# Linear attention feeding a squared-ReLU MLP on one core: the front of the kernel reordered and its loads and stores spread over three queues

## Chip, cores and metric

One Trainium2 chip, one of its cores. The metric is device time in microseconds of one execution; the kernel before takes 1178.36 us (median of 3 runs, 1177.33 to 1179.15). What is said of stages comes from one profiled execution.

## What is computed

For each of 8 batches and 8 heads (sequence 576, head dimension 64, float32):

```
kv  = k^T v                                  # 64 x 64 for each head
o   = q kv;   o = o / sqrt(mean(o^2) + 1e-6) * g_norm
x   = o, heads side by side                  # 4608 tokens x 512
out = (s * relu(x @ w_in)^2 + b) @ w_out     # 512 -> 2048 -> 512
```

w_in (512 x 2048) and w_out (2048 x 512) arrive as 64-bit floats: the kernel reads each as two 32-bit words and makes a float32 of it. Because b is one number, the part of it that reaches the output is b times the column sums of w_out.

## The kernel before, in words

The 4608 tokens are 36 chunks of 128; four chunks make a unit, so there are 9 units. Four groups of two batches (g = 0 to 3) share one pair of kv tables each; a group has 9 chunks, so groups begin at chunks 9, 18 and 27, which belong to the attention that is worked out beside units 1, 3 and 5.

**Attention of a chunk** (`attention`, L277) has three steps: `turn` transposes q on TensorE (L286) and ScalarE copies it out of PSUM (L288); `product` multiplies by the block-diagonal kv (L295), then squares (ScalarE L304), sums (VectorE L306), takes the root (L308), inverts (L310) and scales (L312); `turn_x` transposes the result (L320) into xT (L323). `x_sums` (L329) makes four sums of quarters of xT. `kv_product` (L253) multiplies k and v of a pair of heads in 64 x 64 pieces (L262); after the fourth pair ScalarE copies the kv into `bd_kv` (L273). `load_kv` (L89) loads k and v of a head with two DMAs each, all on SP's queue, into a pool of four buffers for k and four for v; `load_q` (L99) loads two chunks of q with four DMAs.

**The two multiplications** of a unit use Strassen-Winograd products, seven in place of eight: quarters and sums of quarters on both sides. The first one (`mm1`, L364) runs over four blocks s of w_in, with seven slots each: x1, z2, x6, y7, x5, x3, y4; each slot is four matmuls, which the trace shows as eight records, and slots x3 and y4 of a block come between the slots of the next block, so that 26 slots form the stretch and the last two follow later. ScalarE and VectorE evict the banks (L161, L362, L374, L406, L407). The second one (`mm2`, L432) has 14 slots (seven products times two row blocks), reads the seven combinations of w_out from DRAM through a ring of three 1 MB buffers (`load_w2`, L424) and stores the output rows (L459).

**The weights.** `load_w` (L116) brings a block of two 128-row (or 128-column) strips of w into one of two raw buffers, with two DMAs of 512 KB on SP's queue. `round_w` (L133) converts a block: ScalarE scales the high words (L148) and the low words (L149); VectorE then shifts the high words and masks the sign away (L151), puts the sign back (L155) and adds the low words (L158). `make_w_in(s)` (L169) converts two blocks and makes three sums, which stay in SBUF. `make_w_out(s)` (L200) converts two blocks into `up` and `dn` (one buffer each), makes four differences (one of them, t3, in the place of a quarter of `up`), adds the block's rows to `wsum` (L161) and stores the seven combinations to DRAM (L220, SP's queue). When all four blocks are done, `bias_row` (L244) multiplies wsum by b on TensorE. `send_w` (L546) loads the next raw block in a fixed order: w_in's blocks, then w_out's.

**The order** is written out by hand, and each engine and each DMA queue works its own list in that order. At the start (L551 to L569): two raw blocks of w, k and v of heads 0 to 3, q of two chunks, k and v of heads 4 to 7, q of two more chunks, four kv pairs, w_in's block s = 0, attention of chunks 0 to 3, x_sums. Then the units (L592): unit 0 converts w_in's blocks s = 1, 2, 3 after slots 0, 6 and 12 of the first multiplication (L630) and all of w_out, s = 0 to 3, between its two multiplications (L620), then loads the ring. The side work (`side_of`, L571), attention for the next unit's chunks and, in units 1, 3 and 5, the four kv pairs in one piece, is spread over the second multiplication's slots by a due time (L614). The loads of heads 0 to 3 of a new group go out at the start of the unit that needs them (L616), those of heads 4 to 7 after the first and second pair (L637).

## Time and profile before

| what | value |
|---|---|
| time, median of 3 runs | 1178.36 us |
| the profiled execution: time, span | 1181.61 us, 1179.8 us |
| granted TensorE clock, mean | 0.939 |
| busy: TensorE, VectorE, ScalarE, GpSimd | 1010.7, 480.9, 203.4, 2.5 us |
| DMA: moved, mean rate | 128.86 MB, 109 GB/s |
| HBM read, written | 111.15 MB, 16.78 MB |

How to read the lines shown further on. A line of a timeline gives the start in us, the length, the engine, the line of the kernel, the operation, output <- input, the shape and how many instructions are merged (x16), and in brackets how long the engine had idled and what ended that. SPq, ACTq and POOLq are the issuing of DMAs by SyncE, ScalarE and GpSimd: their length is that of the issue and not of the transfer. A line of windows gives for each stretch its length, the busy time of PE (matmul), PEld (weight load), DVE (VectorE), ACT (ScalarE) and POOL (GpSimd) with the number of instructions, the granted TensorE clock, the mean busy share of the 16 DMA engines and the rate. A line of groups gives total busy time, mean ns of one, then the idle time before them with its releaser. A line of waits gives total us, how often, and the longest. A float32 matmul shows as two records.

### The profile page before, as it was taken

What the parts mean: (1) busy time and instruction counts of PE and PEld (TensorE: products, weight loads), DVE (VectorE), ACT (ScalarE), POOL (GpSimd) and SP (SyncE); (2) the same over time, 40 slices, a digit from 0 to 9 for tenths busy, and PEclk for the clock granted to TensorE, in tenths of its full rate; (3) what the DMA queues carried; (4) which work ended last, traced back from release to release, by engine and by line L of the source; (5) the groups of instructions that cost most, each with busy time, mean ns of one, the idle gap of its engine ahead of it and who ended that gap; (6) DMA issues with size and microseconds to landing.
All of it is one profiled execution on the core that took longest, in us unless ns stands there. A gap on an engine that the chain in (4) does not pass through costs nothing.

```text
span 1179.8 us, 14111 instructions
## 1 busy us (share of the span) xinstructions
PE 1010.7 (86%) x6050; PEld 869.3 (74%) x6050; DVE 480.9 (41%) x765; ACT 203.4 (17%) x338; POOL 2.5 (0%) x8
## 2 busy tenths in 40 slices
PE   2588100799978999999979999998699999999998
PEld 2467100688867888888768888887588888888887
DVE  0469565234431355244414452443044534433541
ACT  0353221011101111111111111111011111111100
POOL 0000000000000000000000000000000000000000
PEclk9999655799998999999979999999799999999999
DMA  7434445336133401270245023602350234034022
GB/s 219 138 90 143 130 147 177 151 108 204 55 103 122 142 37 72 81 219 31 81 143 179 1 77 129 197 9 99 117 178 1 81 126 116 16 127 144 1 74 104
DMA packets 79855, 128.86 MB, mean 109 GB/s; under 512 B 43056, under 2 KB 55344, under 8 KB 71728
## 3 DMA queue, kind: packets, MB, share of 16 engines
q1 hardware_dynamic: 79344, 127.95, 33.5%
q8 instruction: 48, 0.79, 0.3%
q14 instruction: 15, 0.12, 0.0%
q10 hardware_dynamic: 448, 0.00, 0.0%
HBM read 111.15 MB, written 16.78 MB: 108 GB/s over the span
## 4 chain that ended last, share of the span: by engine, by line
PE 76%; DVE 10%; SPq 5%; DMA 5%; issue 2%; ACT 2%; DVEq 0%; ACTq 0%
PE x_ps L84 42%; PE y_ps L84 23%; PE z_ps L84 5%; SPq L93 4%; PE x_ps L295 3%; PE xT_ps L320 2%; DVE a L164 2%; DMA w_raw<-in_moe_w_out_dram 2%; PE qT_ps L286 1%; DMA v_sb<-in_v_dram 1%; PE kv_ps L262 1%; DVE wsum L161 1%; DVE xn L312 1%; SPq L220 1%; DVE ss L306 1%
## 5 line engine op out<-in xcount | busy, mean ns | idle before, releaser
L84 PE MATMUL x_ps<-w_sb,a 128*128 128x256 f32 x864 | 200.6, 386 | 9.7 <-DMA w_sb<-w 9.7
L84 PEld LDWEIGHTS x_ps<-w_sb,a 128*128 128x128 f32 x864 | 164.3, 193 | 35.6 <-issue 13.8
L84 PE MATMUL y_ps<-w_sb,a 128*128 128x256 f32 x720 | 162.5, 381 | 0.0
L84 PEld LDWEIGHTS y_ps<-w_sb,a 128*128 128x128 f32 x720 | 135.1, 191 | 17.5 <-issue 0.2
L84 PE MATMUL y_ps<-xs,wb 128*128 128x256 f32 x576 | 136.4, 380 | 0.7 <-DVE a L161 0.7
L84 PE MATMUL x_ps<-xs,ws 128*128 128x256 f32 x576 | 136.2, 379 | 0.0
L374 ACT COPY r<-x_ps 128x512 f32<-128x512 f32 x108 | 63.2, 585 | 343.7 <-PE x_ps L84 338.8
L84 PEld LDWEIGHTS x_ps<-xs,ws 128*128 128x128 f32 x576 | 109.4, 190 | 15.2 <-ACT r L374 0.4
L84 PEld LDWEIGHTS y_ps<-xs,wb 128*128 128x128 f32 x576 | 109.0, 191 | 15.6 <-DVE a L161 1.1
L161 DVE TENSOR_TENSOR a<-y_ps,r 128x512 f32<-128x512 f32 x72 | 49.5, 687 | 130.4 <-ACT r L374 130.4
L444 DVE SCALAR_TENSOR_TENSOR or<-x_ps,s_col,b_row 128x256 f32<-128x256 f32 x54 | 26.1, 484 | 148.3 <-PE x_ps L84 148.3
L262 PE MATMUL kv_ps<-v_sb,k_sb 64*64 64x64 f32 x1152 | 40.0, 279 | 49.9 <-DMA v_sb<-in_v_dram 49.7
L362 DVE SCALAR_TENSOR_TENSOR a<-a 128x512 f32<-128x512 f32 x108 | 74.7, 692 | 3.7
L262 PEld LDWEIGHTS kv_ps<-v_sb,k_sb 64*64 64x64 f32 x1152 | 34.3, 187 | 55.8 <-issue 43.0
L84 PE MATMUL z_ps<-xT,wa 128*128 128x256 f32 x288 | 70.1, 387 | 4.5 <-DVE a L161 4.5
L306 DVE TENSOR_REDUCE ss<-sq 128x8 f32<-128x512 f32 x36 | 24.6, 684 | 120.9 <-ACT sq L304 120.9
L84 PE MATMUL x_ps<-xT,wa 128*128 128x256 f32 x288 | 69.6, 385 | 0.0
L84 PE MATMUL b_ps<-wsum,b_sq 128*128 128x512 f32 x2 | 2.1, 1140 | 77.9 <-DVE wsum L161 77.9
L84 PE MATMUL x_ps<-w_sb,s 128*128 128x256 f32 x288 | 68.5, 393 | 0.0
L84 PE MATMUL x_ps<-xT,ws 128*128 128x256 f32 x288 | 68.0, 379 | 0.0
L84 PEld LDWEIGHTS z_ps<-xT,wa 128*128 128x128 f32 x288 | 55.7, 194 | 13.5 <-DVE a L161 5.7
L84 PEld LDWEIGHTS x_ps<-w_sb,s 128*128 128x128 f32 x288 | 55.5, 197 | 8.7 <-issue 1.2
(65 smaller groups left out, 797.4 us busy)
## 6 DMA issues: line engine op xcount, KB each, us to landing
w_sb<-w SPq DMA_DIRECT2D x63, 1024.0 KB, 4.9
k_sb<-in_k_dram SPq DMA_DIRECT2D x64, 144.0 KB, 2.9
v_sb<-in_v_dram SPq DMA_DIRECT2D x64, 144.0 KB, 3.0
q_sb<-in_q_dram SPq DMA_DIRECT2D x72, 128.0 KB, 4.8
out_dram<-o SPq DMA_DIRECT2D x36, 256.0 KB, 2.2
w_raw<-in_moe_w_in_dram SPq DMA_DIRECT2D x16, 512.0 KB, 4.7
w_raw<-in_moe_w_out_dram SPq DMA_DIRECT2D x16, 512.0 KB, 6.3
w<-w_t SPq DMA_DIRECT2D x12, 256.0 KB, 3.2
```

The costliest lines, as they stand in the source:

```text
L84: nc.tensor.matmul(o, lhsT=lhsT, rhs=rhs, start=start, stop=stop, skip_group_check=True)
L93: nc.sync.dma_start(out=t[s * HB : s * HB + HB].rearrange("p j d -> p (j d)"), in_=src[2 * g + s, h].rearrange("(p j) d -> p (j d)", j=R),)
L161: nc.vector.tensor_tensor(out=o, in0=a, in1=b, op=ALU.add)
L164: nc.vector.tensor_tensor(out=o, in0=a, in1=b, op=ALU.subtract)
L220: nc.sync.dma_start(out=w2_dram[i][:, 2 * s : 2 * s + 2, :], in_=src)
L262: nc.tensor.matmul(kv_ps[g][s][l * HB : l * HB + HB, p, :], lhsT=kt[rows, j, :], rhs=vt[rows, j, :], start=(j == 0), stop=(j == R - 1),)
L295: nc.tensor.matmul(ps[half, p, :], lhsT=st["qT"][:, p, half], rhs=bd[:, s, p, :], start=True, stop=True,)
L306: nc.vector.reduce_sum(ss, sq, axis=mybir.AxisListType.X)
L320: nc.tensor.transpose(ps[:, p, :], st["xn"][:, 2 * p : 2 * p + 2, :], ident)
L362: nc.vector.scalar_tensor_tensor(t, t, 0.0, t, ALU.max, ALU.mult)
L374: nc.scalar.copy(st[name], src)
L444: nc.vector.scalar_tensor_tensor(o, ps, s_col, other, ALU.mult, ALU.add)
```

## The change

- **Conversion.** The scaling of the high words becomes a Prelu whose slope for negative numbers makes the scaled number positive and sets, after VectorE's shift, the sign bit. VectorE's mask and the operation L155 go.
- **Column sums.** VectorE no longer adds up wsum. `bias_row` multiplies each row strip of `up` and `dn` by b on TensorE as soon as it is converted and accumulates in one PSUM bank (16 matmuls of 128 x 512 instead of one).
- **w_out.** Block s = 0 is converted inside unit 0's first multiplication, after slot 18 (x5 of s = 2); s = 1 to 3 after its end. The seven stores go out on GpSimd's queue, two of them after the upper block, five after the lower.
- **w_in.** Upper and lower blocks of s = 0 are converted among the attention of chunks 2 and 3; those of s = 1 to 3 after slots 0, 4 and 11.
- **Start.** k of all eight heads first on SP's queue, v on ScalarE's, into a pool of their own that is given back for `gp` afterwards; then q, a raw block, q, a raw block. The products of chunks 0 to 3 use the banks of the first multiplication.
- **Later units.** The side work has fixed slots. The kv pairs of units 1, 3 and 5 stand after slots 4, 9, 14 and 19 of the first multiplication. Heads 0 to 3 are loaded one unit ahead; unit 0 puts its q loads and these kv loads after the last raw block and ahead of the ring's first load.

```diff
     qp = ctx.enter_context(tc.tile_pool(name="qp", bufs=2))
     attp = ctx.enter_context(tc.tile_pool(name="attp", bufs=2))
     xp = ctx.enter_context(tc.tile_pool(name="xp", bufs=2))
-    gp = ctx.enter_context(tc.tile_pool(name="gp", bufs=NS))
     rp = ctx.enter_context(tc.tile_pool(name="rp", bufs=2))
     dram = ctx.enter_context(tc.tile_pool(name="dram", bufs=1, space=bass.MemoryType.DRAM))
     ps_t = ctx.enter_context(tc.tile_pool(name="ps_t", bufs=2, space=bass.MemoryType.PSUM))
...
     kv_in, q_in, w_raw = {}, {}, {}
-    def load_kv(g, h):
-        for name, src in (("k", k), ("v", v)):
-            t = kvp.tile([P, R, D], FP32, name=f"{name}_sb", tag=name)
+    def load_kv(g, h, pool=kvp, queues=(nc.sync, nc.sync)):
+        for name, src, queue in zip("kv", (k, v), queues):
+            t = pool.tile([P, R, D], FP32, name=f"{name}_sb", tag=name)
             for s in range(2):
-                nc.sync.dma_start(
+                queue.dma_start(
                     out=t[s * HB : s * HB + HB].rearrange("p j d -> p (j d)"),
                     in_=src[2 * g + s, h].rearrange("(p j) d -> p (j d)", j=R),
                 )
...
         raw = w_raw.pop(i).rearrange("p b n -> p (b n)")
         dst = dst.rearrange("p b n -> p (b n)")
         if not wide:
             nc.vector.tensor_copy(out=dst, in_=raw)
             return
-        hi = raw.bitcast(FP32).rearrange("p (n two) -> p n two", two=2)[:, :, 1]
-        lo = raw.rearrange("p (n two) -> p n two", two=2)[:, :, 0]
-        nc.scalar.activation(hi, hi, AF.Copy, scale=2.0**-112)
+        pairs = raw.rearrange("p (n two) -> p n two", two=2)
+        hi, lo = raw.bitcast(FP32).rearrange("p (n two) -> p n two", two=2)[:, :, 1], pairs[:, :, 0]
+        nc.scalar.activation(hi, hi, AF.Prelu, scale=2.0**-112, alpha=-(2.0**32))
         nc.scalar.activation(lo, lo, AF.Copy, scale=2.0**-29)
-        yb, db = raw.rearrange("p (n two) -> p n two", two=2)[:, :, 1], dst.bitcast(U32)
+        db = dst.bitcast(U32)
         nc.vector.tensor_scalar(
-            out=db, in0=yb, scalar1=3, scalar2=0x7FFFFFFF,
-            op0=ALU.logical_shift_left, op1=ALU.bitwise_and,
-        )
-        nc.vector.scalar_tensor_tensor(
-            db, yb, 0x80000000, db, ALU.bitwise_and, ALU.bitwise_or
+            out=db, in0=pairs[:, :, 1], scalar1=3, scalar2=None, op0=ALU.logical_shift_left
         )
         nc.vector.tensor_tensor(out=db, in0=db, in1=lo, op=ALU.add)
...
     wa, wb, ws = {}, {}, {}
-    def make_w_in(s):
-        wa[s] = wp.tile([P, 2, DM], FP32, name=f"wa_{s}")
-        wb[s] = wp.tile([P, 2, DM], FP32, name=f"wb_{s}")
+    def round_w_in(s, lower):
+        store, base = (wb, FC // 2) if lower else (wa, 0)
+        store[s] = wp.tile([P, 2, DM], FP32, name=f"w{'ab'[lower]}_{s}")
+        round_w(base + 2 * s, store[s])
+    def sum_w_in(s):
         ws[s] = wp.tile([P, 3, 2, HN], FP32, name=f"ws_{s}")
-        round_w(2 * s, wa[s])
-        round_w(FC // 2 + 2 * s, wb[s])
         a11, a12 = wa[s][:, :, :HN], wa[s][:, :, HN:]
         a21, a22 = wb[s][:, :, :HN], wb[s][:, :, HN:]
         s1, s2, s4 = (ws[s][:, i] for i in range(3))
         add(s1, a21, a22)
+        sub(s2, s1, a11)
         sub(a21, a11, a21)
-        sub(s2, s1, a11)
         sub(s4, a12, s2)
     def w_in_of(i, s, b, c):
...
     w2_dram = {i: dram.tile([P, FC // 2, HN], FP32, name=f"w2_{i}") for i in range(1, 8)}
-    wsum = const.tile([P, DM], FP32, name="wsum")
     def make_w_out(s):
         up = convp.tile([P, 2, DM], FP32, name="w_up", tag="up")
         dn = convp.tile([P, 2, DM], FP32, name="w_dn", tag="dn")
         t = convp.tile([P, 3, 2, HN], FP32, name="w_t", tag="wt")
-        round_w(FC + 2 * s, up)
-        round_w(FC + FC // 2 + 2 * s, dn)
         b11, b12 = up[:, :, :HN], up[:, :, HN:]
         b21, b22 = dn[:, :, :HN], dn[:, :, HN:]
         t1, t2, t4 = (t[:, i] for i in range(3))
         t3 = b12
+        def keep(*which):
+            for i, src in which:
+                nc.gpsimd.dma_start(out=w2_dram[i][:, 2 * s : 2 * s + 2, :], in_=src)
+        round_w(FC + 2 * s, up)
+        bias_row(up, s == 0, False)
         sub(t1, b12, b11)
-        if s == 0:
-            nc.vector.tensor_copy(out=wsum, in_=up[:, 0])
-        for m, b in ((up, 0), (up, 1), (dn, 0), (dn, 1)):
-            if (s, b) != (0, 0) or m is dn:
-                add(wsum, wsum, m[:, b])
-        sub(t3, b22, b12)
+        keep((1, b11), (5, t1))
+        round_w(FC + FC // 2 + 2 * s, dn)
+        bias_row(dn, False, s == NS - 1)
         sub(t2, b22, t1)
         sub(t4, b21, t2)
-        for i, src in ((1, b11), (2, b21), (6, t2), (7, t3), (5, t1), (3, b22), (4, t4)):
-            nc.sync.dma_start(out=w2_dram[i][:, 2 * s : 2 * s + 2, :], in_=src)
+        sub(t3, b22, b12)
+        keep((2, b21), (6, t2), (3, b22), (4, t4), (7, t3))
     ident = const.tile([P, P], FP32, name="ident")
...
     nc.vector.tensor_scalar(out=b_sq, in0=b_sq, scalar1=b_col, scalar2=None, op0=ALU.mult)
     b_row = const.tile([P, DM], FP32, name="b_row")
-    def bias_row():
-
-        ps = ps_t.tile([P, DM], FP32, name="b_ps", tag="t")
-        matmul(ps, b_sq, wsum, True, True)
-        nc.scalar.copy(b_row, ps)
+    b_ps = []
+    def bias_row(w, first, last):
+        if first:
+            b_ps.append(ps_t.tile([P, DM], FP32, name="b_ps", tag="t"))
+        for b in range(2):
+            matmul(b_ps[0], b_sq, w[:, b], first and b == 0, last and b == 1)
+        if last:
+            nc.scalar.copy(b_row, b_ps[0])
     kv_ps = {}
...
     xT = {}
-    def attention(c):
+    def attention(c, first=False):
         bd = bd_kv[c // R % 2]
...
             nc.scalar.copy(st["qT"], ps)
         def product():
-            ps = ps_a.tile([P, NP, P], FP32, name="x_ps", tag="x")
+            if first:
+                ps = bank_of("att", "xy"[c % 2]).rearrange("p b (m n) -> p (b m) n", m=2)
+            else:
+                ps = ps_a.tile([P, NP, P], FP32, name="x_ps", tag="x")
             for p in range(NP):
                 for s in range(2):
                     half = slice(s * HB, s * HB + HB)
...
             load_w(blocks[sent[0]])
             sent[0] += 1
-    for _ in range(2):
-        send_w()
-    for h in range(4):
-        load_kv(0, h)
+    kv0p = tc.alloc_tile_pool(name="kv0p", bufs=H)
+    for h in range(H):
+        load_kv(0, h, kv0p, (nc.sync, nc.scalar))
     load_q(0)
-    for h in range(4, H):
-        load_kv(0, h)
+    send_w()
     load_q(2)
+    send_w()
     for p in range(NP):
         kv_product(0, p)
-    make_w_in(0)
+    kv0p.release()
+    gp = ctx.enter_context(tc.tile_pool(name="gp", bufs=NS))
+    turn, product, turn_x = zip(*(attention(c, True) for c in range(4)))
+    turn[0]()
+    turn[1]()
+    product[0]()
+    turn[2]()
+    product[1]()
+    turn[3]()
+    turn_x[0]()
+    round_w_in(0, False)
     send_w()
+    product[2]()
+    turn_x[1]()
+    product[3]()
+    turn_x[2]()
+    round_w_in(0, True)
     send_w()
-    first = [attention(c) for c in range(4)]
-    for n in range(6):
-        for i in range(2, -1, -1):
-            if 0 <= n - i < 4:
-                first[n - i][i]()
+    turn_x[3]()
     x_sums(0)
+    sum_w_in(0)
     def side_of(u):
         if u + 1 >= U:
-            return []
-        chunks = range(4 * u + 4, 4 * u + 8)
-        todo = []
-        for c in chunks:
-            if c % R == 0:
-                todo.append([lambda p=p, g=c // R: kv_product(g, p) for p in range(NP)])
-            todo += [[a] for a in attention(c)]
-        todo.append([lambda: x_sums(u + 1)])
-        return todo
-
-    def side_loads(u):
+            return {}
+        turn, product, turn_x = zip(*(attention(c) for c in range(4 * u + 4, 4 * u + 8)))
+        return {
+            2: [turn[0]],
+            3: [product[0]],
+            4: [turn[1]],
+            5: [turn_x[0], product[1]],
+            6: [turn[2]],
+            7: [turn_x[1], product[2]],
+            8: [turn[3]],
+            9: [turn_x[2], product[3]],
+            11: [turn_x[3]],
+            12: [lambda: x_sums(u + 1)],
+        }
+    kv_due = {c // 4 - 1: c // R for c in range(R, CH, R)}
+    def loads(u):
         if u + 1 < U:
-            c = 4 * u + 4
-            load_q(c)
-            load_q(c + 2)
-
-    kv_due = {c // 4 - 1: c // R for c in range(R, CH, R)}
+            load_q(4 * u + 4)
+            load_q(4 * u + 6)
+        if u + 1 in kv_due:
+            for h in range(4):
+                load_kv(kv_due[u + 1], h)
     for u in range(U):
+        if u > 0:
+            loads(u)
         steps = [mm1(u, s) for s in range(NS)]
         slots = []
         for s in range(NS):
...
             if b:
                 slots.append(b["y4"])
             slots += [a["x6"], a["y7"], a["x5"]]
-        m1 = len(slots)
-        second = mm2(u)
-        slots += [second[0], steps[-1]["x3"], steps[-1]["y4"]] + second[1:]
-        side_loads(u)
-        todo = side_of(u)
-
-        at = [0.0]
-        for n in range(len(slots)):
-            at.append(at[-1] + (2.0 if n > m1 + 2 else 1.0))
-        lo, hi = at[m1 + 2], 0.95 * at[-1]
-        due = [lo + (hi - lo) * i / max(1, len(todo) - 1) for i in range(len(todo))]
-        done = 0
-        if u in kv_due:
-            for h in range(4):
-                load_kv(kv_due[u], h)
         for n, slot in enumerate(slots):
-            if u == 0 and n == m1:
-                for s in range(NS):
-                    make_w_out(s)
+            slot()
+            if u == 0:
+                if n in (0, 4, 11):
+                    s = (0, 4, 11).index(n) + 1
+                    for lower in (False, True):
+                        round_w_in(s, lower)
+                        send_w()
+                    sum_w_in(s)
+                if n == 18:
+                    make_w_out(0)
                     send_w()
                     send_w()
-                tc_late()
-                bias_row()
-                load_w2(0, 0)
-                load_w2(0, 1)
-            slot()
-            if u == 0 and n in (0, 6, 12):
-                make_w_in(n // 6 + 1)
+            elif u in kv_due and n % 5 == 4 and n < 20:
+                p = n // 5
+                kv_product(kv_due[u], p)
+                if p < 2:
+                    for h in (4 + 2 * p, 5 + 2 * p):
+                        load_kv(kv_due[u], h)
+        if u == 0:
+            for s in range(1, NS):
+                make_w_out(s)
                 send_w()
                 send_w()
-            while done < len(todo) and due[done] <= at[n + 1]:
-                for m, step in enumerate(todo[done]):
-                    step()
-                    if len(todo[done]) > 1 and m < 2:
-                        for h in (4 + 2 * m, 5 + 2 * m):
-                            load_kv(kv_due[u], h)
-                done += 1
-        assert done == len(todo)
+            loads(0)
+            tc_late()
+            load_w2(0, 0)
+            load_w2(0, 1)
+        second, side = mm2(u), side_of(u)
+        for n, slot in enumerate(second):
+            slot()
+            if n == 0:
+                steps[-1]["x3"]()
+                steps[-1]["y4"]()
+            for step in side.get(n, []):
+                step()
 # ---- launch: one core; inputs and outputs as the reference has them ----
```

## The prediction

> **What bounds the kernel now.** I read the page first, then the windows cut at the stages, then the waits, then the timelines of the stages that lose time.
>
> ```profile
> span 1179.8 us, 14111 instructions
> PE 1010.7 (86%) x6050; PEld 869.3 (74%) x6050; DVE 480.9 (41%) x765; ACT 203.4 (17%) x338; POOL 2.5 (0%) x8
> PEclk9999655799998999999979999999799999999999
> ```
>
> TensorE is busy for 86% of the span; the rest of the time has a place. The clock row dips after the start and three times later. The windows, cut where unit u's first product starts, show what the dips belong to (columns: length, then busy time of PE, PEld, DVE, ACT, POOL, then clock, DMA share, GB/s):
>
> ```profile
> 0.00:68.58 68.58, 28.40 (x385) 22.67 (x386) 15.62 (x25) 14.64 (x24) 2.48 (x8) 1.00 0.59 161
> 68.58:123.46 54.88, 49.75 (x210) 41.28 (x208) 47.92 (x63) 21.53 (x27) 0.00 (x0) 0.94 0.36 115
> 123.46:213.13 89.67, 2.07 (x3) 0.53 (x3) 46.52 (x58) 18.35 (x18) 0.00 (x0) 0.52 0.51 169
> 213.13:276.77 63.64, 63.36 (x336) 53.85 (x337) 23.10 (x42) 9.17 (x17) 0.00 (x0) 0.95 0.33 122
> 276.77:402.94 126.17, 115.89 (x834) 100.04 (x833) 44.48 (x74) 19.45 (x36) 0.00 (x0) 0.95 0.36 113
> 402.94:508.53 105.59, 105.32 (x546) 91.25 (x545) 44.48 (x74) 17.98 (x32) 0.00 (x0) 1.00 0.27 90
> 508.53:632.74 124.21, 115.56 (x833) 99.80 (x832) 44.50 (x74) 19.44 (x36) 0.00 (x0) 0.95 0.36 115
> 738.33:868.19 129.86, 117.50 (x834) 101.24 (x833) 44.49 (x74) 19.45 (x36) 0.00 (x0) 0.93 0.35 110
> ```
>
> Read downwards: 68.6 us before the first product; 54.9 us for unit 0's first multiplication; 89.7 us in which TensorE does 2 us of work while w_out is converted; 63.6 us for its second multiplication. A later unit takes 105.59 us with TensorE never idle (105.32), except units 1, 3 and 5, which hold a kv product: (126.17 + 124.21 + 129.86) - 3 x 105.59 = 63.5 us more. So three places can give time: the front, the w_out stage, the three kv units. The waits name their causes:
>
> ```profile
> ACT w_raw L148 <- DMA w_raw<-in_moe_w_out_dram: 53.6, 6, 17.9
> PE kv_ps L262 <- DMA v_sb<-in_v_dram: 49.7, 26, 14.1
> ```
>
> **The kv units.** Two heads' products (72 records) take half of the first row below when TensorE is warm, and 2.15 us and more when it is cold (second row, 66 records):
>
> ```profile
> 341.62 2.58 PE L262 MATMUL kv_ps<-v_sb,k_sb 64*64 64x64 f32 x144
> 20.55 2.15 PE L262 MATMUL kv_ps<-v_sb,k_sb 64*64 64x64 f32 x66 [0.39 <-DMA v_sb<-in_v_dram]
> 16.80 1.23 SPq L93 DMA_DIRECT2D v_sb<-in_v_dram  x2
> v_sb<-in_v_dram SPq DMA_DIRECT2D x64, 144.0 KB, 3.0
> ```
>
> Heads 4 to 7 are now asked for only when heads 0 to 3 are used up; at 0.62 us an issue (third row), their 16 loads alone take 10 us with TensorE standing. The change puts the four pairs behind first-multiplication slots 4, 9, 14 and 19. The pair of slot 4 frees the buffers that are needed at slot 14, ten slots (17 us, pitch below) for eight issues (5 us) and the landing (3.0, fourth row): covered. The first four heads are asked for one unit earlier. The four ACT copies behind slot 19 (1.51 us, below) have six slots until the unit's second multiplication; without that cover they would add their 1.5. So I charge 1.29 us a pair plus 0.15 for the changes of shape, 5.8 us a unit; bounds 4.8 us (1.2 each) and 10.8 us (cold, 2.7 each). Three units: 17.4 instead of 63.5, a gain of 46.1. The side work (attention beside the second multiplication) gets two slots instead of one between product and last turn, which takes out the 0.27 us idle of each of seven units (105.59 - 105.32): 1.9 us. What ran from 276.77 to 1179.8, 903.0 us, becomes 855. Edits that only rename, reorder two subtractions or move a pool cost nothing.
>
> **The front.** Rows of its parts:
>
> ```profile
> 30.72 1.23 SPq L93 DMA_DIRECT2D v_sb<-in_v_dram  x2
> 36.30 1.51 ACT L273 COPY bd_kv<-kv_ps 64x256 f32<-64x256 f32 x4 [34.29 <-PE kv_ps L262]
> 51.41 1.98 PE L295 MATMUL x_ps<-bd_kv,qT 128*64 128x128 f32 x16
> 53.31 1.12 PE L286 MATMUL qT_ps<-ident,q_sb 128*128 128x128 f32 x4
> 56.32 1.09 PE L320 MATMUL xT_ps<-ident,xn 128*128 128x128 f32 x4 [1.89 <-DVE xn L312]
> 68.58 3.42 PE L84 MATMUL x_ps<-xT,wa 128*128 128x256 f32 x8
> 402.94 1.89 PE L84 MATMUL x_ps<-xT,wa 128*128 128x256 f32 x8
> 404.66 1.89 PE L84 MATMUL z_ps<-xT,wa 128*128 128x256 f32 x8
> 10.00:20.00 10.00, 3.75 (x78) 3.19 (x78) 0.29 (x1) 0.00 (x0) 0.00 (x0) 1.00 0.89 244
> ```
>
> SP issues the last v load at 30.7 now. With w and q behind k, and v on ACT's queue (whose engine idles 34.29 us before the bd_kv copies, so the sixteen issues hold nothing up), k and v are 32 x 147 KB = 4.7 MB; at 244 GB/s for a share of 0.89, so 265 at about 0.97, they land by 2.5 (first issue and latency, my estimate from the 3.0 of a landing) + 17.8 = 20.3. One queue alone would need 0.7 + 32 x 0.62 + 3 = 24. The last pair then ends at 22.5, bd_kv at 24. The Trainium skill (DMA: Bandwidth & Descriptors, Issuing engines are not separate DMA queues) says that a second issuing engine saves only issue time, since all queues run on the same engines; by it too the landing is 20.3 and not half of the 30.7. The trace shows one loaded queue and cannot test it.
>
> Four chunks of attention cost TensorE 4 x (1.12 + 1.98 + 1.09) = 16.8 us cold; the products now use four banks of the first multiplication instead of one. Chunks 2 and 3 have their q behind the first w block and wait 1.5 us; conversions in ACT's and DVE's order cost another 1.5. First product at 24 + 19.8 = 43.8, against 68.58.
>
> **Unit 0, first multiplication.** The conversion loses one of three DVE passes:
>
> ```profile
> L148 ACT ACTIVATE w_raw<-w_raw 128x1024 f32<-128x1024 f32 x16 | 18.3, 1142 | 57.5 <-DMA w_raw<-in_moe_w_out_dram 53.6 <-DMA w_raw<-in_moe_w_in_dram 3.6 <-DVE a L362 0.2
> L151 DVE TENSOR_SCALAR w_up<-w_raw 128x1024 uint32<-128x1024 uint32 x4 | 2.8, 692 | 30.6 <-ACT w_raw L148 30.6
> L155 DVE SCALAR_TENSOR_TENSOR w_up<-w_raw,w_up 128x1024 uint32<-128x1024 uint32 x4 | 4.9, 1226 | 0.1
> L158 DVE CUSTOM_DVE_ANT_0 w_up<-w_raw,w_up 128x2048 uint16<-128x2048 uint16 x4 | 4.9, 1225 | 0.5
> L161 DVE TENSOR_TENSOR wsum<-wsum,w_up 128x512 f32<-128x512 f32 x7 | 4.8, 689 | 0.1
> L84 PE MATMUL b_ps<-wsum,b_sq 128*128 128x512 f32 x2 | 2.1, 1140 | 77.9 <-DVE wsum L161 77.9
> ```
>
> A block costs 0.69 + 1.23 = 2.0 us with its gap instead of 3.2; Prelu is taken at the 1.14 of Copy (as many elements). TensorE needs 19 slots of 1.73 us (404.66 - 402.94) up to slot 18: 32.8, 2 cold, 2.6 behind w_in's sums and ACT: 81.2. There make_w_out(0) now stands **with its bias matmuls in TensorE's order**, so TensorE waits for DVE. DVE's queue from 45.5 (w_in of s = 0 converted): sums 5.4; three w_in pairs at 4.0 + 2.7 = 20.0; the evictions up to slot 18, 22 operations of 0.69 = 15.2 (two each for z2, x5 and y4, three for x3); the upper block 2.0. Sum 88. So TensorE stands about 7 us, cools, and does two bias matmuls at 2.1 us (two records each, last row), then the lower pair at half that: 94.3. Seven slots (12.1) end at 107, against 123.46. Without that stall it would be 93.4, the lower bound; cold throughout, 109.
>
> **w_out, s = 1 to 3, and the wait for the ring.**
>
> ```profile
> 161.14 2.33 SPq L130 DMA_DIRECT2D w_raw<-in_moe_w_out_dram  x4
> 168.18 1.14 ACT L148 ACTIVATE w_raw<-w_raw 128x1024 f32<-128x1024 f32 x1 [17.22 <-DMA w_raw<-in_moe_w_out_dram]
> 182.45 0.57 SPq L220 DMA_DIRECT2D w<-w_t  x1
> 183.12 2.29 SPq L130 DMA_DIRECT2D w_raw<-in_moe_w_out_dram  x4
> 208.03 1.28 SPq L426 DMA_DIRECT2D w_sb<-w  x3
> 160.00:170.00 10.00, 0.00 (x0) 0.00 (x0) 0.65 (x1) 1.82 (x2) 0.00 (x0) 0.50 0.98 316
> 1.24 1.84 POOL L229 MEMSET bd_kv<- 128x1024 f32 x2
> ```
>
> Now a cycle is 22.0 us (161.14 to 183.12): load 7.0, then conversion and sums on DVE until the last store goes out at 182.45, and the next loads stand in SP's queue behind that store. With the stores on POOL's queue the loads go out when a raw buffer comes free. DVE's part falls to 2 x 2.0 + 4 x 0.69 = 6.8, the column sums (4 x 0.69) leaving it for a TensorE that is idle here. But the next upper block overwrites t3's buffer, so it waits for the last store, and 2.1 MB of loads and 1.84 MB of stores share the engines. No DMA of POOL is in the trace: its price lies between SP's 0.57 and a few us (2.5 in rival 1); I take 0.92, a POOL memset, the nearest row of that engine. Cycle about 14. s = 1 ends at 116, s = 3 at 144.
>
> Then the **new wait**: SP has eight q and sixteen kv loads of unit 1 queued ahead of the first w2 load; TensorE and all of unit 0's second multiplication wait for that. Issue alone: 130 + 24 x 0.63 + 5 = 150. By bytes from 111 on: 4.2 MB raw, 5.5 stores, 3.4 q and kv, 1.05 w2 = 14.2 MB at 300 GB/s (316 at best) = 47 us: 158. I take 157, nearer the bytes; ends 147 (cover holds) and 167. That replaces 213.13: 56 us gained. Afterwards 63.6 us as before.
>
> **Sum.** 157 + 63.6 + 855 = 1075.6 of span against 1179.8: 104 us less. The profiled execution took 1181.6, so 1077.4; it lies 3.25 above the median of 1178.36, so **1074 us**.
>
> **The rivals.**
>
> 1. *The stores on POOL keep the w_out cycle long.* For: seven a cycle in one in-order queue, of which the last decides; POOL has no DMA row. Against: only 21 after the first multiplication. At 2.5 us each plus landing the cycle stays at 22 and w2 starts near 183: 1100. The Trainium skill (SBUF — State Buffer, SBUF: two separate sides) has a rule that speaks for this: a DMA issued by GpSimd cannot have its descriptors written while VectorE runs a two-port operation. L151 moves 1024 elements in 0.69 us where L155 takes 1.23, which looks like such a mode; by the rule a store would be delayed by 0.69 at most, two a cycle, 4 us over three cycles. Chance 0.13.
> 2. *The kv products cost what they cost now.* If loads came late again behind slot 14, or cold products returned (10.8 us a unit and 10 us of waits), the kv units keep 45 us more of their excess: 1119. Against: DMA share in these stretches is 0.27 to 0.36. Chance 0.04.
> 3. *Prelu is not in the table that is resident.* Then each change between it and Sqrt loads a table, 1.28 us by the row below; some five such changes in the front, 6 to 10 us: 1082. The change would then not do only what it says. Chance 0.08.
>
> ```profile
> L80 ACT ACT_TABLE_LOAD x1 | 1.3, 1283 | 0.7 <-PEq L656 0.7
> ```
>
> 4. *Slower.* One mechanism: a store from POOL blocks its queue. The forecast lies 104 us under the present; 21 stores after slot 25 decide once each takes (104 + 3 x 14) / 21 = 7.0 us; at 8 us the kernel takes 1074 + 21 x 8 - 42 = 1200. Nothing in the profile comes near 7 us for an issue. Chance 0.02.
>
> **How the numbers follow.** The forecast has 0.73, with its own range 1052 to 1095 (w2 start 147 to 167, kv units 14 to 32, the first multiplication 12 faster without the stall). Rivals 1 and 3 stretch it to 1048 to 1102. Times within 0.2% (2.4 us, about what a measurement of this kernel can tell from none) come only if a blocked POOL cancels all: 0.02. Faster 0.95, slower 0.03.
>
> **What would show it.** First product near 44 us; TensorE idle 5 to 8 us before the first bias matmul, near 81; end of the first multiplication near 107; first w2 product near 157 with q and kv loads landing just before it; units 1, 3 and 5 at 111 us, the others at 105.3, clock 1.00 from there on; no second table load; POOL's stores a few us from issue to landing. A w2 start above 175, a kv unit above 120, or tables reloaded would prove the step concerned wrong.

## The result and the profile after

The changed kernel takes 1079.82 us (median of 4 runs, 1078.49 to 1081.30), the kernel before beside it 1177.84 us: a ratio of 0.9168, 95% interval 0.915 to 0.9186, or 98 us less. The profiled execution took 1079.0 us. First its page: span, busy times and the row of clocks.

```profile
span 1076.7 us, 14153 instructions
PE 1006.4 (93%) x6080; PEld 861.5 (80%) x6080; DVE 452.0 (42%) x733; ACT 202.9 (19%) x338; POOL 21.2 (2%) x36
PEclk9898769999999999999999999999999999999999
```

TensorE does the same work (1006.4 us busy, 1010.7 before) in a span that is 103 us shorter. Of the four dips of the clock one deep one is left, at the w_out stage. The windows are cut where they were cut before: at the first product of each unit's first multiplication, for unit 0 also at that multiplication's end and at the start of its second one.

```profile
0.00:44.34 44.34, 23.64 (x385) 19.24 (x385) 9.10 (x18) 13.54 (x24) 2.48 (x8) 0.98 0.76 202
44.34:106.80 62.46, 54.07 (x217) 43.07 (x216) 50.62 (x71) 25.78 (x32) 4.99 (x7) 0.91 0.53 181
106.80:162.19 55.39, 17.65 (x24) 6.68 (x25) 21.14 (x26) 13.74 (x14) 13.77 (x21) 0.69 0.81 280
162.19:223.88 61.69, 61.69 (x336) 53.26 (x337) 23.10 (x42) 9.29 (x17) 0.00 (x0) 0.98 0.31 110
223.88:334.59 110.71, 110.71 (x833) 95.89 (x832) 44.59 (x74) 19.58 (x36) 0.00 (x0) 1.00 0.33 107
334.59:439.68 105.09, 105.09 (x546) 91.65 (x545) 44.49 (x74) 18.11 (x32) 0.00 (x0) 1.00 0.35 113
```

Read against the rows of before: the front 68.58 to 44.34 us, the first multiplication 54.88 to 62.46 (it now holds a block of w_out), the w_out stage 89.67 to 55.39, the second multiplication 63.64 to 61.69; from there to the end 903.0 became 852.8 (1076.7 - 223.88). That is 24.2 - 7.6 + 34.3 + 2.0 + 50.2 = 103.1 us. In unit 1, which holds kv products, TensorE has no idle time at all (110.71 of 110.71); units 3 and 5 take as long.

**The front** by TensorE's timeline, from the last pair of k and v to the first product of the first multiplication, and the windows of the first 20 us:

```profile
23.77 2.60 PE L266 MATMUL kv_ps<-v_sb,k_sb 64*64 64x64 f32 x68 [0.97 <-DMA v_sb<-in_v_dram]
27.15 1.94 PE L290 MATMUL qT_ps<-ident,q_sb 128*128 128x128 f32 x8 [0.78 <-ACT bd_kv L277]
41.34 0.63 PE L327 MATMUL xT_ps<-ident,xn 128*128 128x128 f32 x4 [3.69 <-ACT sq L311]
44.34 3.62 PE L83 MATMUL x_ps<-xT,wa 128*128 128x256 f32 x8
```
```profile
0.00:10.00 10.00, 1.16 (x6) 0.84 (x6) 0.51 (x3) 1.28 (x1) 2.48 (x8) 1.00 0.68 180
10.00:20.00 10.00, 6.38 (x146) 5.15 (x145) 0.00 (x0) 0.00 (x0) 0.00 (x0) 1.00 1.01 251
```

The last pair begins at 23.8, and the way from there to the first product is 20.6 us. The engines are full from 10 us on (share 1.01), at 251 GB/s. SP does not issue back to back there. Up to 21 us it waits, in six pieces, 6.6 us for an earlier load to land before it issues the next load of k, and the last v load lands at 24.1:

```profile
SPq L92 <- DMA k_sb<-in_k_dram: 6.6, 6, 1.9
```

**Unit 0's first multiplication.** TensorE's timeline around slot 18:

```profile
80.25 1.89 PE L83 MATMUL x_ps<-xs,ws 128*128 128x256 f32 x8
88.69 3.78 PE L83 MATMUL b_ps<-w_up,b_sq 128*128 128x512 f32 x4 [6.55 <-DVE w_up L155]
```

Slot 18 ends at 82.1, TensorE stands 6.55 us for VectorE's conversion, and the bias matmuls take it to 94.55.

**The w_out stage and the ring**, by the timelines of GpSimd (the first store of each block, and at 132.17 the last one of s = 2), VectorE, ScalarE, SP's queue and TensorE:

```profile
111.14 0.73 POOL L208 DMA_DIRECT2D w<-w_up  x1 [16.24 <-DVE w_up L155]
124.37 0.69 DVE L152 TENSOR_SCALAR w_up<-w_raw 128x1024 uint32<-128x1024 uint32 x1 [8.60 <-DMA w<-w_up]
126.73 0.73 POOL L208 DMA_DIRECT2D w<-w_up  x1 [9.44 <-DVE w_up L155]
130.28 11.37 SPq L104 DMA_DIRECT2D q_sb<-in_q_dram  x8
132.17 0.71 POOL L208 DMA_DIRECT2D w<-w_up  x1
132.56 1.10 ACT L149 ACTIVATE w_raw<-w_raw 128x1024 f32<-128x1024 f32 x1 [7.39 <-DMA w_raw<-in_moe_w_out_dram]
140.06 0.69 DVE L152 TENSOR_SCALAR w_up<-w_raw 128x1024 uint32<-128x1024 uint32 x1 [8.70 <-ACT w_raw L149]
142.42 0.73 POOL L208 DMA_DIRECT2D w<-w_up  x1 [9.54 <-DVE w_up L155]
152.52 1.23 SPq L92 DMA_DIRECT2D v_sb<-in_v_dram  x2
154.64 1.29 SPq L433 DMA_DIRECT2D w_sb<-w  x3
162.19 5.11 PE L83 MATMUL x_ps<-w_sb,a 128*128 128x256 f32 x16 [13.44 <-DMA w_sb<-w]
```

From block to block it is 15.6 and 15.7 us (111.14, 126.73, 142.42). Before the blocks of s = 2 and s = 3 VectorE waits 8.6 and 8.7 us for the last store of the block before, t3's, because the next upper block is written over t3. The row of s = 3 (140.06) names ScalarE instead, since ScalarE's scaling of the lower block ended last, at 139.9. But the shift of the upper block doesn't need the lower one, and the upper one's high words had been scaled since 133.7 (row of 132.56). The store issued at 132.17 landed at 139.9. SP issues the eight q and sixteen kv loads from 130.28 to 153.75. Then it waits another 0.5 us for the last store of `up`, which lands at 154.25, and only then issues the ring's first load; TensorE's second multiplication waits for that.

```profile
SPq L433 <- DMA w<-w_up: 0.5, 1, 0.5
```

**A kv unit**: one pair between two slots, 1.28 us of records and 1.21 us until the next product (232.61 to 233.82).

```profile
232.61 1.28 PE L266 MATMUL kv_ps<-v_sb,k_sb 64*64 64x64 f32 x72
```

The groups of ScalarE settle Prelu: still one table load, and a Prelu of 1135 ns where Copy took 1142.

```profile
L149 ACT ACTIVATE w_raw<-w_raw 128x1024 f32<-128x1024 f32 x16 | 18.2, 1135 | 24.7 <-DMA w_raw<-in_moe_w_out_dram 21.0 <-DMA w_raw<-in_moe_w_in_dram 3.7
L79 ACT ACT_TABLE_LOAD x1 | 1.3, 1283 | 0.7 <-PEq L682 0.7
```

### The profile page after: what moved, and what is told of

Read it like the earlier page. It is cut to its first block, busy times and chain, and to the rows that moved or that the text cites. A ratio compares the mean times of both kernels' runs of the same rounds, so it can differ in the third digit from the quotient of the medians.

```text
span 1076.7 us, 14153 instructions
## 1 busy us (share of the span) xinstructions
PE 1006.4 (93%) x6080; PEld 861.5 (80%) x6080; DVE 452.0 (42%) x733; ACT 202.9 (19%) x338; POOL 21.2 (2%) x36
## 4 chain that ended last, share of the span: by engine, by line
PE 85%; issue 5%; DMA 4%; DVE 3%; POOL 1%; ACT 1%; SPq 0%; DVEq 0%; POOLq 0%; ACTq 0%
PE x_ps L83 44%; PE y_ps L83 25%; PE z_ps L83 8%; PE x_ps L302 3%; DMA k_sb<-in_k_dram 2%; PE kv_ps L266 2%; PE qT_ps L290 1%; POOL w L208 1%; PE xT_ps L327 1%; DMA w_sb<-w 1%; DMA w<-w_up 1%; DMA w_raw<-in_moe_w_in_dram 1%; DVE wb L155 0%; DMA v_sb<-in_v_dram 0%; DVE ws L161 0%
## 5 line engine op out<-in xcount | busy, mean ns | idle before, releaser
L83 PE MATMUL x_ps<-w_sb,a 128*128 128x256 f32 x864 | 196.8, 383 | 13.4 <-DMA w_sb<-w 13.4
L83 PE MATMUL x_ps<-w_sb,s 128*128 128x256 f32 x288 | 65.8, 382 | 0.0
L83 PEld LDWEIGHTS x_ps<-xT,wa 128*128 128x128 f32 x288 | 55.5, 194 | 8.2 <-issue 0.5
L83 PEld LDWEIGHTS x_ps<-xT,ws 128*128 128x128 f32 x288 | 54.5, 190 | 7.5
L414 DVE TENSOR_TENSOR a<-a 128x512 f32<-128x512 f32 x36 | 24.9, 692 | 79.3 <-ACT a L413 79.3
```

What stands on the lines that cost most here:

```text
L83: nc.tensor.matmul(o, lhsT=lhsT, rhs=rhs, start=start, stop=stop, skip_group_check=True)
L414: nc.vector.tensor_mul(t, t, t)
```

## The experiments

The theory: the gain has three separate places (front, w_out stage, kv units), and what still bounds the w_out stage is first the store that t3's buffer waits for and then SP's list ahead of the ring. The rivals: one of the parts does nothing, or the stage is bound by GpSimd's queue, by bytes alone, or by VectorE. Times are medians of 4 runs; ratios are to the kernel before beside them. The absolute places of the front shift by some 3 us from one profile to the next before any edit acts (first bias matmul at 88.69 after, at 92.03 in ring_first, with the same instructions ahead of it), so distances within a run are compared. Five runs differ from the changed kernel by only 3 to 4 us (vec_sums, wout0_after, one_queue, ring_first, up_two). Their four times lie all below or all above its four, but the intervals of the ratios overlap or touch its own (0.915 to 0.9186), so the size of these differences is rough.

**before_kv**: the kernel before with the new place of the kv products and the earlier load of heads 0 to 3, and nothing else.

```diff
+            if u in kv_due and n % 5 == 4 and n < 20:
+                p = n // 5
+                kv_product(kv_due[u], p)
+                if p < 2:
+                    for h in (4 + 2 * p, 5 + 2 * p):
+                        load_kv(kv_due[u], h)
```

> The kernel before with one part of the change alone: the kv pairs of units 1, 3 and 5 behind slots 4, 9, 14 and 19, heads 0 to 3 loaded one unit ahead (in unit 0 behind the ring's first loads). Theory A (the kv units' part of the gain is independent of the front): units 1, 3 and 5 take 110.7 to 111.5 us instead of 124 to 130, time 1130 to 1135. Rival (the kv units gain only with the fixed side slots or the warm front): units above 115, time above 1145.

Measured 1133.47 us, ratio 0.9609 (0.9586 to 0.9631): 45 us less than 1178.4. The window of unit 1:

```profile
277.23:388.44 111.21, 110.94 (x834) 95.59 (x833) 44.58 (x74) 19.45 (x36) 0.00 (x0) 1.00 0.34 107
```

126.17 became 111.21, and the clock 1.00. So this part alone is worth 45 of the 98 us, nearly independent of the rest.

**kv_piece**: the changed kernel with the four pairs in one piece behind slot 4. It tells the spreading from the mere change of place.

```diff
-            elif u in kv_due and n % 5 == 4 and n < 20:
-                p = n // 5
-                kv_product(kv_due[u], p)
...
+            elif u in kv_due and n == 4:
+                for p in range(NP):
+                    kv_product(kv_due[u], p)
```

> The changed kernel with the four kv pairs of units 1, 3 and 5 in one piece behind slot 4 instead of spread over slots 4, 9, 14 and 19; heads 0 to 3 still come one unit ahead. Theory A (what the spreading gains is the time for the loads of heads 4 to 7): TensorE waits 12 to 16 us in each of the three units and cools, as in the kernel before: time 1115 to 1128. Rival (the early loads of heads 0 to 3 are what counts): time within 6 us of the changed kernel.

Measured 1119.19 us, ratio 0.9488 (0.9467 to 0.9509): 39.4 us of the 45 are lost again. TensorE's timeline in unit 1:

```profile
234.12 2.33 PE L266 MATMUL kv_ps<-v_sb,k_sb 64*64 64x64 f32 x144
239.69 0.41 PE L266 MATMUL kv_ps<-v_sb,k_sb 64*64 64x64 f32 x2 [3.24 <-DMA v_sb<-in_v_dram]
243.04 2.96 PE L266 MATMUL kv_ps<-v_sb,k_sb 64*64 64x64 f32 x70 [0.21 <-DMA v_sb<-in_v_dram]
```

The first two pairs take 2.33 us; then TensorE waits for the loads whose buffers the first pairs held, cools, and works cold (2.96 for 70 records, where 144 took 2.33). It is the spreading that gives the time.

**three_pass**: the sign by Copy, mask and a third VectorE pass, as before.

```diff
-        nc.scalar.activation(hi, hi, AF.Prelu, scale=2.0**-112, alpha=-(2.0**32))
+        nc.scalar.activation(hi, hi, AF.Copy, scale=2.0**-112)
...
+        nc.vector.scalar_tensor_tensor(
+            db, yb, 0x80000000, db, ALU.bitwise_and, ALU.bitwise_or
+        )
```

> The changed kernel with the conversion of the kernel before: Copy instead of Prelu, mask, and VectorE's third pass of 1.23 us. Theory A (VectorE's queue decides at slot 18 and each w_out cycle holds two blocks in series): 7 or 8 more passes before slot 18 make TensorE's stand 7 to 9 us longer, and each of three cycles grows by 2.5: 14 to 17 us more, 1093 to 1097. Rival (the cycles are set by bytes): 7 to 9 us more, 1086 to 1089. If Prelu itself cost a table load, the change would be smaller than both.

Measured 1094.94 us, ratio 0.9279 (0.9257 to 0.9301): 15.1 us lost. TensorE:

```profile
99.01 3.41 PE L83 MATMUL b_ps<-w_up,b_sq 128*128 128x512 f32 x4 [11.92 <-DVE w_up L160]
```

The stand at slot 18 grows from 6.55 to 11.92 us, and the blocks follow one another at 17.2 and 17.9 us. The Prelu is worth 15 us where VectorE's list is what TensorE waits for.

**vec_sums**: the column sums back on VectorE, one pair of matmuls at the end.

```diff
+            nc.vector.tensor_copy(out=wsum, in_=w[:, 0])
+            add(wsum, wsum, w[:, 1])
+        else:
+            for b in range(2):
+                add(wsum, wsum, w[:, b])
```

> The changed kernel with the column sums back on VectorE (four additions of 0.69 us for each s) and one bias matmul at the end, at the places where the bias matmuls stood. Theory A (the bias matmuls in TensorE's order cost the stand of 6.5 us and 6 us of matmuls in the first multiplication; the additions cost 2.8 us in each of the chains of s = 1 to 3): 11 to 12 us won and 8 to 9 lost: time 1076 to 1082, nothing gained by the sums on TensorE. Rival (taking the sums from VectorE is a gain of its own): time 1086 or more.

Measured 1076.82 us, ratio 0.9131 (0.911 to 0.915), 3.0 us less than the changed kernel.

```profile
145.93 2.07 PE L83 MATMUL b_ps<-wsum,b_sq 128*128 128x512 f32 x2 [46.69 <-DVE wsum L158]
```

Without bias matmuls in its order TensorE does not stand at slot 18 at all, which makes up for slower blocks (15.7 and 17.3 us): the first multiplication ends at 99.24 instead of 106.80. At this place in TensorE's order the sums gain nothing; the stall that they bring eats what they save VectorE.

**wout0_after**: the block s = 0 of w_out converted after the first multiplication instead of inside it.

```diff
-                if n == 18:
-                    make_w_out(0)
-                    send_w()
-                    send_w()
...
-            for s in range(1, NS):
+            for s in range(NS):
```

> The changed kernel with block s = 0 of w_out converted after the first multiplication like the others, as in the kernel before. Theory A: TensorE's stand of 6.5 us and the four bias matmuls (6 us) leave the first multiplication, which ends at 94 to 95 instead of 106.8, and one more cycle of 15.7 us follows it: start 3 us later, time 1081 to 1085. Rival (the conversion inside costs more than it saves): start earlier, time under 1078.

Measured 1082.94 us, ratio 0.9183 (0.9153 to 0.9214): 3.1 us more. The second multiplication starts at 165.85 instead of 162.19: the stall is gone and a fourth block is added after the end. With its stall the early block is worth only those 3 us.

**sp_stores** and **act_stores**: the stores of w_out on SP's queue, and those of s = 1 to 3 on ScalarE's. They tell whether GpSimd's queue shortens the cycle, and whether it lengthens the stores.

```diff
-                nc.gpsimd.dma_start(out=w2_dram[i][:, 2 * s : 2 * s + 2, :], in_=src)
+                nc.sync.dma_start(out=w2_dram[i][:, 2 * s : 2 * s + 2, :], in_=src)
```

> The changed kernel with the w2 stores on SP's queue as in the kernel before. Theory A (what GpSimd's queue buys is that raw loads need not stand behind the stores): the raw loads of the next block go out only after the last store; stores land in 3 us, cycle 18 to 20 instead of 15.7: time 1087 to 1093. Rival (stores and loads share the engines, so that it is all one): within 3 us of the changed kernel.

Measured 1088.47 us, ratio 0.9233 (0.9215 to 0.9251): 8.7 us more, inside what was expected, but for another reason. The timelines of TensorE and SP's queue:

```profile
128.39 3.78 PE L83 MATMUL b_ps<-w_up,b_sq 128*128 128x512 f32 x4 [8.97 <-DVE w_up L155]
144.18 3.78 PE L83 MATMUL b_ps<-w_up,b_sq 128*128 128x512 f32 x4 [10.08 <-DVE w_up L155]
149.54 5.64 SPq L104 DMA_DIRECT2D q_sb<-in_q_dram  x8
171.86 6.16 PE L83 MATMUL x_ps<-w_sb,a 128*128 128x256 f32 x16 [21.33 <-DMA w_sb<-w]
```

The cycle is 15.8 us (128.39 to 144.18), as with GpSimd, but another wait sets it: the raw loads stand behind the stores again, and VectorE waits for them until 141.87, when t3's store has long landed (138.34). What is lost comes after the cycles: the 24 q and kv loads stand behind the last store, from 149.54 to 165.42, and the ring behind them. So GpSimd's queue buys the passing of 24 loads beside the conversion and, as long as `up` has one buffer, no shorter cycle.

```diff
-                nc.gpsimd.dma_start(out=w2_dram[i][:, 2 * s : 2 * s + 2, :], in_=src)
+                (nc.gpsimd if s == 0 else nc.scalar).dma_start(out=w2_dram[i][:, 2 * s : 2 * s + 2, :], in_=src)
```

> The changed kernel with the w2 stores of s = 1 to 3 on ScalarE's queue instead of GpSimd's (those of s = 0 stay). Theory A (a store lands late because raw loads run on the same engines): landing stays at 5 to 7 us, cycle 15 to 16, time within 2 us. Rival (late landing belongs to GpSimd's stores): landing 3 us as SP's had in the kernel before, cycle about 12, start 7 us earlier, time near 1073.

Measured 1091.5 us, ratio 0.9257 (0.9224 to 0.929): 11.7 us more, where hardly any change was expected. Of its issues of DMAs, one group; ScalarE's timeline; SP's waits from 147 to 168 us:

```profile
w<-w_t ACTq DMA_DIRECT2D x9, 256.0 KB, 7.1
```
```profile
131.84 1.13 ACT L149 ACTIVATE w_raw<-w_raw 128x1024 f32<-128x1024 f32 x1 [8.12 <-DVE w_t L161]
```
```profile
SPq L92 <- DMA w<-w_dn: 9.1, 1, 9.1
```

A store lands in 7.1 us, as on GpSimd's queue (7.2), so the late landing is not GpSimd's. The time is lost in two other places. ScalarE cannot scale the lower block (131.84) before it has issued a store that waits for VectorE's difference; blocks come at 17 and 17.5 us, which makes 3.2 us. And a v load on SP's queue stands for 9.1 us, until a store has landed that ScalarE issued only at 156.84; from the last block's first store to the ring's first load it is 20.1 us (148.21 to 168.27) instead of 12.2, which makes 7.8.

**one_queue**: k and v of the first group on SP's queue alone.

```diff
-        load_kv(0, h, kv0p, (nc.sync, nc.scalar))
+        load_kv(0, h, kv0p)
```

> The changed kernel with k and v of the first group on SP's queue alone. Theory A (issue at 0.62 us binds one queue): last v issue at 21 to 22 instead of an end of the engines' work near 24; first product 2 to 4 us later than 44.3, time 1081 to 1084. Rival (the engines are full from 10 to 30 us with either, share 0.99 to 1.01): within 1.5 us of the changed kernel.

Measured 1083.56 us, ratio 0.9191 (0.9169 to 0.9213): 3.7 us more. TensorE's timeline:

```profile
24.45 2.15 PE L266 MATMUL kv_ps<-v_sb,k_sb 64*64 64x64 f32 x66 [0.17 <-DMA v_sb<-in_v_dram]
33.29 1.09 PE L290 MATMUL qT_ps<-ident,q_sb 128*128 128x128 f32 x4 [2.05 <-DMA q_sb<-in_q_dram]
47.57 3.62 PE L83 MATMUL x_ps<-xT,wa 128*128 128x256 f32 x8
```

From 10 to 20 us the engines are at share 0.78 instead of 1.01 and at 225 GB/s instead of 251, yet the last pair starts 0.7 us later only (24.45 against 23.77). The 3.2 us of the first product (47.57 against 44.34) come from q, which stands behind all of k and v. The q of chunks 2 and 3 goes out 2.6 us later (25.88 against 23.28): TensorE waits 2.05 us for it, and its next rows stay longer (1.09 and 1.98 us at 33.29 and 34.31, where the changed kernel has 0.65 and 1.09 from 33 us on). The Trainium skill (DMA: Bandwidth & Descriptors, Issuing engines are not separate DMA queues) says that a second issuing engine saves only the time of issuing; the two runs agree, and hardly any of the issuing is saved either: the last of the 32 loads goes out at 21.30 from one list and at 20.05 from two, and the last v load lands at 24.3 and 24.1.

**ring_first**, **up_two**, **ring_up**: two waits at the end of the w_out stage, each taken away alone and then both. The first puts two of the ring's three loads ahead of the q and kv loads; the second gives `up` two buffers, so that t3's store holds nothing up.

```diff
-            loads(0)
...
+            loads(0)
```

> The changed kernel with one edit: the first two loads of the w2 ring are put on SP's queue ahead of unit 1's 24 q, k and v loads instead of behind them. Theory A (the queue and its 3.4 MB stand before the ring): in the changed kernel the last b11 store is issued at 142.4 and a store lands 7 us later, so the ring load can be issued near 150 instead of 154.6 and has no q and kv bytes in front of it: second multiplication of unit 0 starts at 153 to 156 instead of 162.2, time 6 to 9 us less (1071 to 1074). Theory B (bytes bind whatever their order, the engines being full from 130 to 160): start at 160 or later, time within 2 us of the changed kernel. If q now comes too late for the side work, TensorE stands before the first turn beside the second multiplication.

```diff
-        up = convp.tile([P, 2, DM], FP32, name="w_up", tag="up")
+        up = convp.tile([P, 2, DM], FP32, name="w_up", tag="up", bufs=2)
...
-        sub(t1, b12, b11)
-        keep((1, b11), (5, t1))
+        keep((1, b11))
...
+        sub(t1, b12, b11)
+        keep((5, t1))
```

> The changed kernel with two buffers for the upper block of w_out and the difference t1 worked out after the lower block, so that the next upper block needn't wait for the store of t3. Theory A (the landing of t3's store sets the cycle of 15.7 us): the cycle of s = 2 and 3 falls to 12 to 13.5, start of the second multiplication 3 to 6 us earlier, time 1074 to 1077. Rival (the bytes of raw loads and stores set the cycle): cycle 15 to 16, time within 1.5 us of the changed kernel.

> Both edits of the first two kernels together: ring loads ahead of unit 1's q and kv loads, and two buffers for the upper block. Theory A (two waits in series, each hiding the other's gain): the w_out stage ends 9 us earlier as it did with two buffers alone, and the ring load now follows the last store (landing 3 to 5 us) instead of 24 issues: second multiplication of unit 0 starts at 150 to 155, time 1069 to 1073. Rival B (the bytes of the stage decide, whatever the order): start not before 158, time 1075 to 1077.

Measured: ring_first 1076.59 us, ratio 0.913 (0.9099 to 0.9161), 3.2 us less than the changed kernel, between the two expectations; up_two 1076.67, ratio 0.913 (0.9094 to 0.9167), 3.1 less; both together 1069.16, ratio 0.906 (0.9036 to 0.9083), 10.7 less. SP's waits from 135 to 156 us and its timeline in ring_first, timelines of up_two (TensorE, SP's queue) and of ring_up (TensorE):

```profile
SPq L433 <- DMA w<-w_up: 20.9, 2, 14.7
154.84 0.81 SPq L433 DMA_DIRECT2D w_sb<-w  x2
```
```profile
133.43 3.47 PE L83 MATMUL b_ps<-w_up,b_sq 128*128 128x512 f32 x4 [1.53 <-DVE w_up L155]
152.75 26.94 SPq L434 DMA_DIRECT2D w_sb<-w  x5
```
```profile
151.34 5.27 PE L83 MATMUL x_ps<-w_sb,a 128*128 128x256 f32 x16 [10.16 <-DMA w_sb<-w]
```

In ring_first the loads no longer stand behind 24 others and still go out at 154.84: the ring lies where the conversion's buffers lay, and its first load waits 14.7 us, until the last store (issued at 150.35) has landed. In up_two the blocks follow one another at 8.9 and 11.6 us (first bias matmuls at 113.00, 121.85 and 133.43), with the same bytes to move. So t3's store is what held the cycle at 15.7, and not the bytes alone. VectorE's longest waits are now 4.2 and 5.0 us, for the stores of `dn`, which still has one buffer. There the last store goes out at 144.42 (147.86 in the changed kernel) and the ring's first load still only at 152.75, behind the 24. Each wait hides part of the other's price: 3.2 + 3.1 apart, 10.7 together.

**ring_up_defer**: both, and the bias matmuls of s = 0 behind the last slot, with t3 in a buffer of its own.

```diff
-        bias_row(up, s == 0, False)
+        if s:
+            bias_row(up, False, False)
...
+            bias_row(held[0], True, False)
+            bias_row(held[1], False, False)
```

> The kernel ring_up with the four bias matmuls of w_out's block s = 0 taken out of the first multiplication's order on TensorE (they follow its last slot; t3 gets a buffer of its own so that nothing overwrites what they read). Theory A (TensorE's stand of 6.5 us at slot 18 is only the bias matmuls' wait for VectorE): no stand, first multiplication ends at 94 to 98 instead of 107, whole stage 8 to 10 us earlier than in ring_up: time 1060 to 1064. Rival (VectorE or the raw loads are late anyway): under 4 us less than ring_up.

Measured 1061.63 us, ratio 0.8996 (0.8975 to 0.9017), 18.2 us less than the changed kernel. TensorE:

```profile
93.00 1.89 PE L83 MATMUL x_ps<-xs,ws 128*128 128x256 f32 x8
94.72 1.88 PE L83 MATMUL b_ps<-w_up,b_sq 128*128 128x512 f32 x4
142.35 6.31 PE L83 MATMUL x_ps<-w_sb,a 128*128 128x256 f32 x16 [10.01 <-DMA w_sb<-w]
```

No stand at slot 18: the last slot ends at 94.9 instead of 106.80 (the prediction had 93.4 for the case without the stall), and the second multiplication starts at 142.35. This is the fastest of all versions run.

## Why the prediction was right, and where its steps were not

The forecast was 1074 us with a range of 1048 to 1102; 1079.82 lies in it, 5.8 above. The span came out at 1076.7 where the sum gave 1075.6. The steps in turn:

- **kv units: right.** 111 and 105.3 us forecast, 110.71 and 105.09 measured; 855 for what follows unit 0's second multiplication, 852.8 measured. The charge of 5.8 us a unit was 5.6 (110.71 - 105.09). before_kv and kv_piece show the cause. Rival 2 (1119) did not happen, but kv_piece, 1119.19, shows that it was real: it is what the products cost without the spreading.
- **The front: total right (43.8, measured 44.34), its two terms both wrong.** k and v were to have landed at 20.3 and bd_kv to be there at 24: the last pair starts at 23.77, and TensorE goes on at 27.15. The rate of 265 GB/s was carried up from a queue at share 0.89; the full engines gave 251, and 180 in the first 10 us. The attention, put at 19.8, took 17.2 (27.15 to 44.34): TensorE was warm from 33 us on (rows of 0.63 and 1.09 us where I charged 1.12 and 1.98), so its work was less than 16.8 us, though conversions in ScalarE's order cost 3.7 at one place where I had 1.5. The landing is the term that failed. The last v load lands at 24.1 and not at 20.3, hardly earlier than from one queue (24.3 in one_queue, where the prediction had 24), because the loads of both queues wait for earlier ones to land. Two errors of some 3 us cancel; that the total is right is luck.
- **The stall at slot 18: right.** Slot 18's end 81.2 (82.1), stand 7 (6.55), bias matmuls to 94.3 (94.55), end at 107 (106.80). ring_up_defer shows what it costs, three_pass how it grows with VectorE's list.
- **The w_out cycle: the wait was right, its length too short.** 14 us forecast, 15.6 and 15.7 measured; s = 3 ended at 147 instead of 144. That the next upper block waits for t3's store is shown by up_two. Of the 15.7 us, 7.8 lie between the first shift of a block and that store's issue (124.37 to 132.17), and 7.7 are its landing, for which the sum had no term of its own. I had put the fall from 22.0 partly to the stores' leaving SP's queue. sp_stores falsifies that for the kernel as it stands: with the stores on SP the cycle is 15.8. The fall is VectorE's part. With raw loads behind the stores in both kernels, the time from a block's first shift to its last store's issue is 13.1 us before (169.35 to 182.45) and 7.2 in sp_stores (126.06 to 133.25), which is 5.9 of the 6.2. Two third passes (2.5 us) and four sums (2.8) a cycle left VectorE. Put back one at a time, where t3's store also counts, they return 1.6 to 2.2 us (three_pass) and 0 to 1.6 (vec_sums); both together were not tried.
- **The ring: mechanism right, price too low.** "Issue alone: 130 + 24 x 0.63 + 5 = 150" was the lower bound, 157 the choice, 162.19 the measurement. The loads began at 130.28 as forecast, but took 23.5 us to issue and not 15.1, most of it in the eight q loads (11.4), with the engines full; and the first product came 7.5 us after the ring's first issue and not 5. By bytes I had 14.2 MB at 300 GB/s; the window shows 280. What the prediction did not see is the second wait behind this one, the ring's place under the last store: in the changed kernel it ends 0.5 us after the queue is free, and in ring_first it is all that is left. The profile of before had it too: its ring's first load goes out at 208.03, just after the last store has landed (207.95).
- **Second multiplication** 61.69 instead of 63.6.
- **Between span and median: 4.7 of the 5.8 us.** I took 3.25 us off because the profiled execution of before lay that far above its median. That did not carry over: the profiled execution of after took 1079.0, its median is 1079.82. A difference of one execution from its median is scatter and no term of a sum.

Mis-sized terms of the span, late and early: +5.2 at the ring's start (162.19 against 157), of which 3 were there at the end of s = 3; -1.9 in the second multiplication, -2.2 in the units. Sum +1.1 (1076.7 - 1075.6).

Of the rivals, 1 (GpSimd's stores bound the cycle) is false: an issue took 0.57 to 0.73 us (the very first 1.17) against the 0.92 I took and the 2.5 of the rival, and the same stores on SP left the cycle as it was. Its sentence that VectorE delays a store fits one issue, by 0.3 us; the reverse was seen more often (below). Rival 3 (a second table) is false: one load. Rival 4 is false by the same issue times.

**Open**: why the places of the front differ by some 3 us between profiles of kernels that are alike up to there; what makes some issues of q loads long (below); and how the 24 us of the front divide over its edits, since only one_queue takes one of them away. A second buffer for `dn` as well, where ring_up still waits, was not tried.

## What to carry to other kernels

A product that waits for its own loads is worth spreading when its buffers are few: the same four pairs cost 1.4 us each between slots of a warm TensorE, and in one piece the kernel lost 39 us. A gain of only 3 us from taking one wait away does not say that the wait is harmless: look who waits behind it, and take both away in one run before giving up either. A cycle of the same length is not the same wait (15.7 us here, 15.8 in sp_stores), and where a row names who ended a wait, ask whether the waiter needs that instruction. Before moving small work to an idle engine, look what its place in that engine's order makes wait: the sums on TensorE freed 2.8 us a block of VectorE and cost a stand of 6.55 us at slot 18.
